# A transformer block on one Trainium2 core: the opening put in order by hand, the end by halves

## The chip, the core and the metric

The kernel runs on one core of a Trainium2 chip. The core has a matrix engine (TensorE, PE in the profile; its weight loads are listed as PEld), a vector engine (VectorE, DVE), a scalar engine (ScalarE, ACT), a general engine (GpSimd, POOL) and a queue for transfers (SyncE, SP). Each engine executes its own instructions strictly in the order in which the program issues them, and semaphores join them. Data stands in SBUF, matrix products arrive in PSUM, and transfers run on 16 DMA engines; SP issues nearly all of them here, and ACT can issue them too. An engine that issues a transfer waits first for the semaphores that the transfer needs, and what is queued behind it waits as well.

The metric is the device time of one execution in microseconds (us). An execution of the kernel before takes 1185.17 us, the median of three runs.

## The reference

The block normalises x (2048 tokens of 576 numbers, no learned scale), and adds to x two branches that both read the normalised x: attention over eight keys at distances 0, 2, ... 14 in 32 heads of 18, and a feed-forward layer of 4608 with a ReLU.

```python
def reference(A_x, A_wqkv, A_wo, B_x, B_w1, B_w2):
    def _A_ref(x, wqkv, wo):
        ...
        qkv = (lambda x, *d: x.transpose(*d))((x @ wqkv).reshape(B, S, 3, H, Dh), 2, 0, 3, 1, 4)
        ...
        attn = _softmax(logits, axis=-1)
        o = jnp.einsum("bhsw,bhswd->bhsd", attn, vg)
        return (lambda x, *d: x.transpose(*d))(o, 0, 2, 1, 3).reshape(B, S, D) @ wo

    def _B_ref(x, w1, w2):
        h = jnp.einsum("bsd,df->bsf", x, w1)
        zero = jnp.zeros_like(h)
        h = jnp.maximum(h, zero)
        return jnp.einsum("bsf,fd->bsd", h, w2)

    x = A_x
    xn = _layernorm(x, axis=-1)
    return x + _A_ref(xn, A_wqkv, A_wo) + _B_ref(xn, B_w1, B_w2)
```

All inputs are float32.

## The kernel before

**Precision.** Products run in fp32r. So each operand is split into a high half, a copy of type fp32r made by ACT, and a low half, the difference of the number and its high half, made by DVE. A product is three products: high by high, low by high, high by low. The 576 rows of the contraction are four blocks of 128 and a rest of 64; the rest's high and low halves share one block of 128 rows. `TERMS` (L294) lists the 14 products of one output tile as pairs of an x block and a weight block: four high by high, four x-low by weight-high, one for the rest, then five with the weight's low half.

**Tiling.** The tokens come in two phases (even and odd ones). A phase has 1024 tokens: eight token tiles of 128, or four blocks `tb` of 256. The feed-forward layer has 36 blocks of 128 hidden units, three to a chunk, 12 chunks. A slot is one hidden block on one token block; `slots` (L464) runs over phases, chunks, token blocks and the three blocks of a chunk. So slots 0 to 2 are token block 0 (token tiles 0 and 1), slots 3 to 5 block 1 (tiles 2 and 3), 6 to 8 block 2, 9 to 11 block 3.

**A slot's work.** `h_mm(n)` (L467) makes the 14 first products into the PSUM tile `ph`, 256 columns each; ACT takes their ReLU as the high half `hhi` and DVE the low half `hlo`. `o_mm(n)` (L482) makes 12 second products of 288 columns into two PSUM tiles `po`, one for each token tile; after the third slot of a chunk DVE adds the sums to x's tile (L500), and after the last chunk `done` sends the tile out on SP's queue (L461). `ps_o` has two buffers, `ps_h` two, `ps_m` two.

**A token tile's way.** `load_x` brings it in; `stats` (L239) takes mean and variance on DVE, and the negative mean and the root on POOL (L249, L250); `norm` (L254) normalises, on DVE in one instruction or on ACT in two (L258, L259), and ACT copies the last 64 columns once more beside themselves (L263); `make_xt` (L285) transposes it by five products (L275, L276) and splits the transposed tile into its high half (ACT, L278, L280) and low half (DVE, L279, L281). A block's first products need both of its tiles transposed and split.

**Weights.** W1, W2, wqkv and wo come through four staging tiles `st` of 640 columns. `stage_more` loads up to three ahead on SP's queue; `run_splits(n)` splits what is due by step n with `two` (L143): the high half on ACT, the low half on DVE. The due steps of the first chunk are `HEADW` (L32); those of the first wqkv tiles begin at step 2. A W1 tile is loaded by three transfers: 256 KB and twice the 32 KB of the rest's 64 rows.

**The order.** The program is written in the order of its issue: at step n it runs due splits, `h_mm(n + 2)`, the work that `at` has put there, `o_mm(n)`, the work that `late` has put there, and attention's DVE work as far as two counters of modelled time for PE and DVE allow. The opening (L555 to L577) loads x and the first weights, prepares token tiles 0 to 2, and puts tiles 3 to 7 into steps -2 to 5 by the table `HEAD` (L34). The attention's first products (qkv) begin at step 7. 24 transposes of a constant tile (L105) run on PE while the first data is on its way.

Of the kernel before, what the change touches and what calls it, by code (L numbers as in the profile page):

```python
# [17 lines left out]
P = 128  # L18
# [13 lines left out]
HEADW = (-5, -2, -1, 0, 0, 1)  # L32

HEAD = (  # L34
    (-2, 0, 'stats', 3),
    (-2, 1, 'xt', 2, True),
    (-1, 0, 'stats', 4),
    (-1, 1, 'norm', 3, True),
    (0, 0, 'xt', 3, False),
    (0, 0, 'norm', 4, True),  # L40
    (0, 0, 'stats', 6),
    (0, 1, 'stats', 5),
    (1, 1, 'norm', 5, False),
    (1, 1, 'xt', 4, False),
    (2, 1, 'xt', 5, False),
    (2, 1, 'norm', 6, True),
    (2, 1, 'stats', 7),
    (4, 0, 'norm', 7, True),
    (4, 1, 'xt', 6, False),
    (5, 1, 'xt', 7, False),  # L50
# [6 lines left out]
def tile_body(ctx: ExitStack, tc: tile.TileContext, x, wqkv, wo, w1, w2, out):  # L57
# [77 lines left out]
    def run_splits(n):  # L135
        while staged and staged[0][0] <= n:
            _, split, st = staged.popleft()
            split(st)
            stage_more()

    held = None

    def two(hi, lo, src, n):  # L143
        def rest():
            nc.vector.tensor_tensor(lo, src, f32(hi), op=ALU.subtract)  # L145
            dve(n)

        nc.scalar.activation(hi, src, AF.Copy)  # L148
        if held is None:
            rest()  # L150
        else:
            held.append(rest)
# [3 lines left out]
    def w1_task(step, key, f):  # L156
        def load(st):
            c = slice(f * P, (f + 1) * P)
            nc.sync.dma_start(
                st[:, 0:512].rearrange("p (k c) -> p k c", k=KT),  # L160
                w1[0 : KT * P, c].rearrange("(k p) c -> p k c", p=P),
            )
            nc.sync.dma_start(st[0:DR, 512:640], w1[KT * P : D, c])
            nc.sync.dma_start(st[DR:P, 512:640], w1[KT * P : D, c])

        def split(st):
            w = w1p.tile([P, 2, 5 * P], F32R, name="w1t")
            two(w[:, 0, :], w[:, 1, :], st[:, :], 640)
            W1[key] = w

        split_task(step, load, split)

    def w2_task(step, key, f):
        def load(st):
            nc.sync.dma_start(st[:, 0:D], w2[f * P : (f + 1) * P, :])
# [78 lines left out]
    def norm(ph, i, act=False):  # L254
        nm, r = MR.pop((ph, i))
        xn = tmp.tile([P, 640], F32, name="xn", bufs=3)
        if act:
            nc.scalar.activation(xn[:, 0:D], X[ph, i], AF.Identity, bias=nm)  # L258
            nc.scalar.activation(xn[:, 0:D], xn[:, 0:D], AF.Copy, scale=r)  # L259
        else:  # L260
            nc.vector.tensor_scalar(xn[:, 0:D], X[ph, i], nm, r, op0=ALU.add, op1=ALU.mult)
# [4 lines left out]
    def transpose_split(src, last, hi, mix, lo, free=False):  # L266

        if free:
            pa, pb = (ps_o.tile([P, 2, 512], F32, name="po")[:, 0, :] for _ in range(2))
            pa, pb = pa.rearrange("p (k c) -> p k c", k=KT), pb[:, 0:P]  # L270
        else:
            pa = ps_m.tile([P, KT, P], F32, name="pm")
            pb = ps_m.tile([P, P], F32, name="pm")
        for k in range(KT):
            nc.tensor.transpose(pa[:, k, :], src[:, k * P : (k + 1) * P], ident)  # L275
        nc.tensor.transpose(pb, last, ident)  # L276
        t["pe"] += 5 * 0.06
        nc.scalar.activation(hi, pa, AF.Copy)  # L278
        nc.vector.tensor_tensor(lo, pa, f32(hi), op=ALU.subtract)  # L279
        nc.scalar.activation(mix, pb, AF.Copy)  # L280
        nc.vector.tensor_tensor(mix[DR:P], pb[DR:P], f32(mix[DR:P]), op=ALU.subtract)  # L281
        dve(512)
        dve(128)

    def make_xt(ph, i, free=False):  # L285
# [5 lines left out]
        transpose_split(xn[:, 0:512], xn[:, 512:640], d[:, 0:4, :], d[:, 4, :], d[:, 5:9, :], free)  # L291
# [175 lines left out]
    def h_mm(n):  # L467
        ph, c, tb, f = slots[n]
        w, xt = W1[ph, c, f], XT[ph, tb]
        pt = ps_h.tile([P, TBN], F32, name="ph")  # L470
        for j, (a, b) in enumerate(TERMS):
            wb = w[:, b // 5, (b % 5) * P : (b % 5 + 1) * P]
            mm(pt, wb, xt[:, a, :], j == 0, j == len(TERMS) - 1, TBN)
# [7 lines left out]

    def o_mm(n):  # L482
        ph, c, tb, f = slots[n]
        hi, lo = H.pop(n)
        w = W2[ph, c, f]
        for k in range(2):
# [3 lines left out]
            for j, (l, b) in enumerate(((hi, 0), (hi, 1), (lo, 0))):  # L490
                for h in range(2):
                    mm(
                        PO[k][:, h, 0:D2], l[:, cs], w[:, b, h * D2 : (h + 1) * D2],
                        f == 0 and j == 0, f == C - 1 and j == 2, D2,
                    )
        if f == C - 1:
# [57 lines left out]

    load_x(0, 0, 2)  # L555
    load_x(0, 1)
    for i in range(1, AHEAD + 1):
        stage_more(i)
        load_x(0, 1 + i)
    for i in range(AHEAD + 2, NI):  # L560
        load_x(0, i)
    stats(0, 0)
    stats(0, 1)
    held = []
    run_splits(-5)
    norm(0, 0)
    norm(0, 1)
    stats(0, 2)
    make_xt(0, 0)
    make_xt(0, 1, True)  # L570
    for f in held:
        f()
    held = None
    run_splits(-LAG)
    norm(0, 2, True)
# [3 lines left out]
    for n in range(-LAG, len(slots)):  # L579
# [38 lines left out]
```

## Time and profile before

| | us |
|---|---|
| median of three runs | 1185.17 (1184.52 to 1185.62) |
| the profiled execution, its own time | 1184.46 |
| its span, first to last instruction | 1182.7 |
| PE busy in the span | 1174.6 |
| DVE busy | 822.3 |
| ACT busy | 306.9 |
| POOL busy | 40.1 |
| first product of h_mm(0) | 9.11 |
| first product of h_mm(6) | 31.54 |
| last product's end | 1178.72 |
| last add's end | 1179.51 |
| last output's issue and landing | 1179.54, 1181.65 |

Times are from the start of the span. The execution's own time is 1.8 us longer than the span, for what lies around it. A row of the timeline gives start, duration, engine, line, operation, and out<-in with partitions and elements. A row of the groups gives the count after x, then the busy time in us, the mean of one in ns, and the idle time before them with what ended it. The chain of waits is followed back from the last instruction: at each step to what released it.

### The profile page before, as it was taken

The numbers are of one execution on the slowest core, as the hardware profiler recorded it, in microseconds if no ns is written. First come the engines' busy times: TensorE is split into PE (matmuls) and PEld (weight loads), VectorE is DVE, ScalarE is ACT, GpSimd is POOL, SyncE is SP. The second block draws the span as 40 slices with busy tenths as digits, with TensorE's granted clock in tenths as the row PEclk, the third lists the DMA queues.
The fourth block names the chain that finished last, engine by engine and source line by source line (L and its number), as shares of the span: only waits on it lengthen the run. The fifth ranks groups of instructions, "written<-read, shape, count | busy, mean of one in ns | idle before, by whom it ended". The sixth has DMA issues, their size and how long they took to land.

```text
span 1182.7 us, 21731 instructions
## 1 busy us (share of the span) xinstructions
PE 1174.6 (99%) x8936; PEld 1164.9 (98%) x8936; DVE 822.3 (70%) x1301; ACT 306.9 (26%) x758; POOL 40.1 (3%) x63
## 2 busy tenths in 40 slices
PE   8999999999999999999999999999999999999998
PEld 8999999999999999999999999999999999999998
DVE  7516885888687668877673288758777884787852
ACT  5422222131222211322233123121322222222210
POOL 2000000010000000000020000000100000000000
PEclk9999999999999999999999999999999999999999
DMA  5312121130312211356342122121302213114541
GB/s 174 85 32 79 39 84 47 47 108 1 99 45 58 65 55 44 104 112 148 105 131 74 47 55 80 32 77 27 98 21 80 70 43 89 47 30 110 115 100 60
DMA packets 137364, 86.16 MB, mean 73 GB/s; under 512 B 48832, under 2 KB 120768, under 8 KB 137264
## 3 DMA queue, kind: packets, MB, share of 16 engines
q1 hardware_dynamic: 134736, 76.58, 24.0%
q10 hardware_dynamic: 2528, 8.20, 2.4%
q8 instruction: 70, 1.15, 0.4%
q14 instruction: 30, 0.25, 0.1%
HBM read 66.58 MB, written 9.96 MB: 65 GB/s over the span
## 4 chain that ended last, share of the span: by engine, by line
PE 95%; DVE 2%; DMA 2%; ACT 0%; SPq 0%; issue 0%; POOL 0%; DVEq 0%; ACTq 0%
PE ph L114 37%; PE po L114 37%; PE pm L114 20%; DMA st<-in_w 1%; DMA xn<-turned 1%; PE pm L275 0%; DVE pr L382 0%; DMA turned<-tr 0%; DVE x L500 0%; DMA x<-in_x 0%; DVE pr L345 0%; SPq L424 0%; DVE w1t L145 0%; DVE w2t L145 0%; DVE bst L245 0%
## 5 line engine op out<-in xcount | busy, mean ns | idle before, releaser
L114 PE MATMUL ph<-xT,w1t 128*128 128x256 f32 x4032 | 513.0, 278 | 1.3 <-ACT xT L278 0.6
L114 PEld LDWEIGHTS ph<-xT,w1t 128*128 128x128 f32 x4032 | 491.9, 188 | 2.1 <-ACT xT L278 0.8
L114 PE MATMUL po<-w2t,hhi 128*128 128x288 f32 x2304 | 400.7, 296 | 0.6 <-DVE w2t L145 0.3
L114 PEld LDWEIGHTS po<-w2t,hhi 128*128 128x128 f32 x2304 | 336.9, 188 | 2.4 <-issue 0.5
L476 ACT ACTIVATE hhi<-ph 128x256 fp32r<-128x256 f32 x288 | 110.1, 382 | 553.5 <-PE ph L114 538.2
L114 PE MATMUL po<-w2t,hlo 128*128 128x288 f32 x1152 | 244.7, 293 | 0.0
L477 DVE SCALAR_TENSOR_TENSOR hlo<-ph,hhi 128x256 fp32r<-128x256 f32 x288 | 121.5, 422 | 161.0 <-ACT hhi L476 160.1
L500 DVE TENSOR_TENSOR x<-po,x 128x576 f32<-128x576 f32 x192 | 143.4, 756 | 69.9 <-PE po L114 67.0
L114 PE MATMUL pm<-wq,xT 128*128 128x432 f32 x896 | 185.5, 358 | 0.0
L114 PEld LDWEIGHTS po<-w2t,hlo 128*128 128x128 f32 x1152 | 183.6, 188 | 0.0
L114 PEld LDWEIGHTS pm<-wq,xT 128*128 128x128 f32 x896 | 163.8, 188 | 5.6
L145 DVE TENSOR_TENSOR w2t<-st,w2t 128x576 fp32r<-128x576 f32 x72 | 54.3, 755 | 45.6 <-ACT w2t L148 45.4
L345 DVE TENSOR_TENSOR pr<-qo,k 128x1152 f32<-128x1152 f32 x64 | 85.8, 1349 | 0.0
L348 DVE TENSOR_REDUCE lg<-pr 128x64 f32<-128x1152 f32 x64 | 84.9, 1343 | 0.0
L375 DVE TENSOR_TENSOR pr<-lg,v 128x1152 f32<-128x1152 f32 x64 | 84.7, 1350 | 0.2
L382 DVE TENSOR_TENSOR pr<-pr 128x288 f32<-128x288 f32 (+1 forms) x128 | 70.6, 601 | 0.1
L145 DVE TENSOR_TENSOR w1t<-st,w1t 128x640 fp32r<-128x640 f32 x72 | 59.0, 820 | 13.8 <-ACT w1t L148 13.7
L148 ACT ACTIVATE w2t<-st 128x576 fp32r<-128x576 f32 x72 | 49.1, 683 | 57.2 <-PE po L114 42.4
L314 ACT ACTIVATE k<-pm 128x144 f32<-128x144 f32 x64 | 18.6, 291 | 143.9 <-PE pm L114 143.9
L148 ACT ACTIVATE w1t<-st 128x640 fp32r<-128x640 f32 x72 | 53.0, 736 | 11.4 <-DMA st<-in_w 11.4
L351 POOL TENSOR_SCALAR_AFFINE_SELECT lg<-lg 1x512 f32<-1x512 f32 x8 | 9.4, 1171 | 844.1 <-DVE lg L348 844.1
L114 PE MATMUL pm<-wq,oT 128*128 128x288 f32 x224 | 35.2, 296 | 0.3 <-ACT oT L438 0.3
(61 smaller groups left out, 444.7 us busy)
## 6 DMA issues: line engine op xcount, KB each, us to landing
st<-in_w SPq DMA_DIRECT2D x72, 288.0 KB, 3.0
st<-in_w SPq DMA_DIRECT2D x72, 256.0 KB, 3.0
st<-in_wqkv SPq DMA_DIRECT2D x32, 216.0 KB, 3.0
turned<-tr SPq DMA_DIRECT2D x64, 80.0 KB, 2.3
xn<-turned SPq DMA_DIRECT2D x16, 320.0 KB, 3.2
st<-in_w SPq DMA_DIRECT2D x144, 32.0 KB, 2.7
out<-x SPq DMA_DIRECT2D x16, 288.0 KB, 2.1
x<-in_x SPq DMA_DIRECT2D x15, 288.0 KB, 3.6
```

The source lines that it names most:

```text
L114: nc.tensor.matmul(o, l, r, start=start, stop=stop)
L145: nc.vector.tensor_tensor(lo, src, f32(hi), op=ALU.subtract)
L148: nc.scalar.activation(hi, src, AF.Copy)
L314: nc.scalar.activation(k[:, W - 1 + i, :], pq[:, 1, :], AF.Copy)
L345: nc.vector.tensor_tensor(pr[i], q, window(k, i), op=ALU.mult)
L348: nc.vector.tensor_reduce(lg[:, i], pr.pop(i).rearrange(heads, d=Dh), axis=AX.X, op=ALU.add)
L351: nc.gpsimd.affine_select(out=z, in_=z, pattern=[[1, NI], [1, W], [0, HG]], compare_op=ALU.is_ge, fill=-1e9 / scale, base=1 - W, channel_m ...
L375: nc.vector.tensor_tensor(pr[i].rearrange(heads, d=Dh), e, window(v, i).rearrange(heads, d=Dh), op=ALU.mult)
L382: nc.vector.tensor_tensor(o, z[:, 0:n], z[:, n : 2 * n], op=ALU.add)
L476: nc.scalar.activation(hi, pt, AF.Relu)
L477: nc.vector.scalar_tensor_tensor(lo, pt, 0.0, f32(hi), op0=ALU.max, op1=ALU.subtract)
L500: nc.vector.tensor_tensor(acc, PO[k][:, :, 0:D2], acc, op=ALU.add)
```

## The change

**The opening is written out by hand**, up to `o_mm(3)` and the transposes of token tile 5; the loop begins at step `FIRST` = 4, and `HEAD` keeps tiles 6 and 7, one step later than before for their transposes.

- The first products of slots 0 and 1 take turns by kind of term (`h_terms`): high by high of slot 0, x-low of slot 0, high by high and x-low of slot 1, then the remaining six of slot 0 and of slot 1. Slot 2's products follow, into a tile of the pool of `po`.
- The second W1 tile is loaded by ACT's queue, behind a small ACT instruction that reads the first half of x's tile 0.
- Token tile 0 is normalised on ACT, tile 1 on DVE; tiles 2 and 3 on DVE by another instruction (`beside`: the root as a second tensor operand).
- The second products of slots 0, 1 and 2 stand ahead of slot 3's first products: `o_mm(0)`, `o_mm(1)`, the transposes of tile 3, `o_mm(2)`, `h_mm(3)`, the transposes of tile 4.
- The low halves of the first two W1 tiles, of the last two W2 tiles of chunk 0 and of two wqkv tiles are made by POOL (`by_pool`) and no longer by DVE.
- The copies of the last 64 columns (L263) go; the transposed rest has 64 rows, and its low half is written from them to the other 64 rows.

**The end.** In the last slot the second products of a token tile are ordered by column half, and each half is added and sent out by itself, the first halves on SP's queue, the second on ACT's.

```diff
-HEADW = (-5, -2, -1, 0, 0, 1)
+HEADW = (-9, -8, -7, -6, -5, -4)
+FIRST = 4
...
+    (4, 0, 'stats', 6),
+    (4, 1, 'norm', 6, True),
+    (4, 1, 'stats', 7),
+    (5, 0, 'norm', 7, True),
+    (5, 1, 'xt', 6, False),
+    (6, 1, 'xt', 7, False),
...
     def two(hi, lo, src, n):
...
+        nc.scalar.activation(hi, src, AF.Copy)
+        if step_now in by_pool:
+            nc.gpsimd.tensor_tensor(lo, src, f32(hi), op=ALU.subtract)
+        else:
             nc.vector.tensor_tensor(lo, src, f32(hi), op=ALU.subtract)
             dve(n)
...
+        elif beside:
+            nc.vector.scalar_tensor_tensor(xn, X[ph, i], nm, r.to_broadcast([P, D]), op0=ALU.add, op1=ALU.mult)
+            dve(600)
...
-        nc.scalar.activation(xn[:, D:640], xn[:, KT * P : D], AF.Copy)
...
+        if end:
+            for k in range(2):
                 for h in range(2):
...
+                    z = X[ph, 2 * tb + k][:, h * D2 : (h + 1) * D2]
+                    nc.vector.tensor_tensor(z, PO[k][:, h, 0:D2], z, op=ALU.add)
+                    (nc.scalar if h else nc.sync).dma_start(o_v[ph, 2 * tb + k][:, h * D2 : (h + 1) * D2], z)
...
+    by_pool.update((-9, -8, -5, -4, 2, 3))
+    both, x_low, w_low, last = TERMS[0:4], TERMS[4:8], TERMS[9:13], [TERMS[8], TERMS[13]]
     load_x(0, 0, 2)
     load_x(0, 1)
...
+    stage_more(1)
+    nc.scalar.activation(spare, X[0, 0][:, 0:1], AF.Copy)
+    queue = nc.scalar
+    stage_more(2)
+    queue = nc.sync
+    load_x(0, 2)
+    stage_more(4)
+    for i in (3, 4, 5):
         load_x(0, i)
     stats(0, 0)
+    norm(0, 0, True)
     stats(0, 1)
+    norm(0, 1)
+    x0 = make_xt(0, 0, parts=True)
+    x0[0]()
+    run_splits(-9)
+    x1 = make_xt(0, 1, True, parts=True)
+    x1[0]()
+    x0[1]()
+    x1[1]()
+    h_terms(0, both)
+    run_splits(-8)
+    load_x(0, 6)
+    load_x(0, 7)
+    stats(0, 2)
+    for z in x0[2:], x1[2:]:
+        for f in z:
+            f()
+    h_terms(0, x_low)
+    h_terms(1, both)
+    h_terms(1, x_low)
+    h_terms(0, w_low + last)
+    h_terms(1, w_low + last)
+    run_splits(-7)
+    norm(0, 2, beside=True)
+    h_out(0)
+    h_terms(2, TERMS, True)
+    h_out(1)
+    run_splits(-6)
+    make_xt(0, 2)
+    h_out(2)
+    stats(0, 3)
+    o_mm(0)
+    run_splits(-5)
+    norm(0, 3, beside=True)
+    o_mm(1)
+    run_splits(-4)
+    make_xt(0, 3)
+    stats(0, 4)
+    norm(0, 4, True)
+    o_mm(2)
+    run_splits(2)
+    h_mm(3)
+    stats(0, 5)
+    make_xt(0, 4)
+    norm(0, 5, True)
+    h_mm(4)
+    run_splits(3)
+    h_mm(5)
+    o_mm(3)
+    make_xt(0, 5)
...
-    for n in range(-LAG, len(slots)):
+    for n in range(FIRST, len(slots)):
```

`h_out(n)` is the second part of `h_mm`: the ReLU on ACT and the low half on DVE. `x0` and `x1` are the four steps of a token tile after its transposes: high half, low half, and the same of the rest. `AHEAD`, the staging tiles and the pools are as before.

More of the change, by code (lines that the diff above doesn't have):

```diff
@@ L271, in transpose_split @@
         else:
             pa = ps_m.tile([P, KT, P], F32, name="pm")
-            pb = ps_m.tile([P, P], F32, name="pm")
+            pb = ps_m.tile([P, P], F32, name="pm")[0:DR]
         for k in range(KT):
             nc.tensor.transpose(pa[:, k, :], src[:, k * P : (k + 1) * P], ident)
-        nc.tensor.transpose(pb, last, ident)
+        nc.tensor.transpose(pb, src[:, KT * P : D], ident)
         t["pe"] += 5 * 0.06
-        nc.scalar.activation(hi, pa, AF.Copy)
-        nc.vector.tensor_tensor(lo, pa, f32(hi), op=ALU.subtract)
@@ L280, in transpose_split, with high, low, last_high @@
[L280 to L285, printed above, removed]
+        def high():
+            nc.scalar.activation(hi, pa, AF.Copy)
+        def low():
+            nc.vector.tensor_tensor(lo, pa, f32(hi), op=ALU.subtract)
+            dve(512)
+        def last_high():
+            nc.scalar.activation(mix[0:DR], pb, AF.Copy)
+        def last_low():
+            nc.vector.tensor_tensor(mix[DR:P], pb, f32(mix[0:DR]), op=ALU.subtract)
+            dve(128)
@@ L286, in make_xt @@
+        steps = high, low, last_high, last_low
+        if not parts:
+            for f in steps:
+                f()
+        return steps
+    def make_xt(ph, i, free=False, parts=False):
         tb, h = divmod(i, 2)
```

106 lines of the change are left out of this document (44 added, 62 removed).

## The prediction

> Short names: T(i) is the five transposes of token tile i, h(n) the 14 first products of slot n (wide, `ph`), o(n) its 12 second products (`po`); "the mark" is the first product of h(6). Durations are rows of the profiled execution, in us; sums by me say so.
>
> **What bounds it now.** First the chain that ended last by share, then the same chain in order of time, to see where TensorE stops waiting.
>
> ```profile
> PE 95%; DVE 2%; DMA 2%; ACT 0%; SPq 0%; issue 0%; POOL 0%; DVEq 0%; ACTq 0%
> ```
>
> ```profile
> 19.42 1.59 PE po L114 x10
> 21.01 1.61 PE ph L114 x14
> ```
>
> From 19.42 on the chain is TensorE alone until the last add, so the time is TensorE's fixed work plus what it loses in the first 20 us and after its last product. An o costs 1.59, an h 1.61, a T 0.55 (0.44 + 0.11 in that chain). Then windows of 3.41 us, for the clock (columns: busy time and instructions of PE, weight loads, DVE, ACT, POOL; granted clock; DMA).
>
> ```profile
> 7.24:10.66 3.42, 2.10 (x14) 1.42 (x13) 3.26 (x9) 3.28 (x10) 0.75 (x2) 1.00 0.96 257
> 10.66:14.07 3.41, 3.41 (x16) 3.19 (x16) 2.17 (x5) 1.50 (x4) 0.00 (x0) 0.50 0.95 314
> 14.07:17.48 3.41, 3.27 (x28) 3.08 (x27) 3.25 (x9) 2.85 (x6) 0.75 (x2) 1.00 0.64 250
> 17.48:20.90 3.42, 3.06 (x21) 2.39 (x20) 3.22 (x8) 3.30 (x9) 1.35 (x2) 1.00 0.28 74
> ```
>
> A window in which PE was 61% busy is followed by one at half clock (a 256-wide product then takes 0.213 instead of 0.114, start to start); 89% busy is followed by full clock. Last, the timeline and the groups, for the steps between transposes and products, and for POOL.
>
> ```profile
> 7.67 0.58 ACT L278 ACTIVATE xT<-pm 128x512 fp32r<-128x512 f32 x1
> ...
> 8.63 0.68 DVE L279 TENSOR_TENSOR xT<-pm,xT 128x512 fp32r<-128x512 f32 x1
> ...
> 17.23 0.81 DVE L245 BATCH_NORM_STATS2 bst<-x 128x6 f32<-128x288 f32 x2
> ...
> 22.73 0.57 POOL L250 TENSOR_TENSOR rstd<-mv,mhalf 128x1 f32<-128x1 f32 x1
> ...
> 31.54 1.66 PE L114 MATMUL ph<-xT,w1t 128*128 128x256 f32 x13
> ```
>
> ```profile
> L351 POOL TENSOR_SCALAR_AFFINE_SELECT lg<-lg 1x512 f32<-1x512 f32 x8 | 9.4, 1171 | 844.1 <-DVE lg L348 844.1
> L307 POOL MEMSET v<- 1x1008 f32 x8 | 7.5, 931 | 0.0
> ```
>
> 31.54 is the mark; T(0) to T(5), h(0) to h(5), o(0) to o(3) lie before it, and in the changed program the same work does. So the change is worth its shift of the mark, plus new waits behind the mark, plus the end.
>
> **To the end of T(2).** ACT now issues the second W1 tile: it waits for x's first half (landed 2.94), issues two, and its third issue has to wait for a semaphore of the first W1 tile's 256 KB (landed 5.52). No ACT issue lies in this stretch; SP's took 0.43 to 0.59, ACT's halo issues (L320) 0.56 to 1.36: I take 0.6, so ACT is free at 6.15 (up to 6.9). The normalisation of tile 0, on ACT now, takes 0.78 + 0.10 + 0.78 (L258, L259): 7.85, against 6.42 on DVE before. T(0) and T(1) start there. ACT then does tile 0's high half (0.59 from 8.65), W1's (0.74), tile 1's (0.59), with starts overlapped by 0.08 as in the timeline: first product at 10.45, 1.3 later than before (9.11). Taking the kinds of terms in turn then does its work: 42 products and a wait of 0.2 for tile 1's low half. PE is about 40% busy in 7.24 to 10.66, so by the row above the next window is at half clock: 16 products to 14.07, 26 more at 0.114 to 17.0, T(2) to 17.5. The low halves of W1 that POOL makes come in time even at 1.5 each (from 9.9: 11.4 and 12.9). What is left to the mark is 3 T, 3 h, 4 o = 1.65 + 4.83 + 6.36 = 12.84. Without any further wait the mark lies at 30.34: a gain of 1.20.
>
> **Wait A, second products.** POOL's queue is in order, and the low half of the second W2 tile stands in it behind the mean and root of tile 3, because `stats(0, 3)` is written ahead of `run_splits(-5)`. Those wait for DVE, whose queue holds tile 2's low halves and h(2)'s low half first. From the end of T(2): tile 2's high half on ACT 0.64 with its handoff, low 0.74, last rows 0.33, hlo(2) 0.45, statistics 0.82 + 0.21 + 0.15 and gaps 1.31, root on POOL 0.66, the W2 split 1.37: 5.50. PE has o(0) and two products of o(1) to do, 1.59 + 0.26; inside, the second half of o(0) also waits for hlo(2), which frees its PSUM tile. PE loses 3.65. The POOL split of 128x576 is in no row: between 0.53 (by the memset, 0.92 ns an element) and 1.9 (the affine select's 2.29 ns an element, 1.32, plus the 0.57 that a one-column tensor_tensor takes). I take 1.32, since the affine select reads and writes too.
>
> **Wait B, T(4).** Tile 4's statistics stand on DVE behind tile 3's low halves, so from the end of T(3): 0.64 + 0.74 + 0.33 + 1.31 + 0.66, then 1.69 on ACT and 0.05: 5.42 until T(4), covered by o(2) and h(3), 3.20. PE loses 2.22. Before, `stats` of 4 was done at 18.5.
>
> **Waits C and D.** T(5) stands directly ahead of h(6), and T(7) ahead of h(9); before, h(5) and o(3), or h(8) and o(6), lay between. In the first products of before the step from the last transpose to the first product was 0.74 (8.37 to 9.11); the next four products wait some 0.17 more for the low half: 0.92 each.
>
> **Clock.** A leaves PE some 40% busy in 20.9 to 24.3, so the window after it runs at half clock: T(3) takes 1.07 instead of 0.55, on the path: 0.55 (0 if the clock stays; 1.6 if the window before is slow too and o(1) with it). The Trainium skill (TensorE: Matmul & The Clock Gate, What's actually happening) has the gate close after an idle window; by that the term is 0 and the sum 1191.1, but the 61% row speaks against it, so the row is used.
>
> **Hidden.** The 16 copies of 64 columns that go (L263, 0.26 each), wq's two splits on POOL and wider normalisations on DVE lie beside PE; DVE has room (9.1 of 10.6 busy to the mark). If that cover were gone the last would cost 0.2 each. On SP the loads of x(6), x(7) and of the third W2 tile now stand behind the second W2 load, which waits for a staging tile that POOL's first split frees (11.4); with the 2.5 to 5.9 from issue to landing seen up to 30 us they are there by 18 to 19, and used after 22.
>
> **The end.** All adds of a token tile wait for its last product, so halves can't start sooner: four adds of 128x288 at 0.45 (L453) against two of 0.76 end 0.33 later. The last output lands 2.1 after its issue (both of the last two did); a half may take less (x: 2.2 against 3.0). Between -0.5 and +0.35; I take +0.2.
>
> **Sum.** -1.20 + 3.65 + 2.22 + 0.92 + 0.92 + 0.55 + 0.2 = +7.26 on 1184.46, this execution's own time (span 1182.7): 1191.7. The three runs lie at 1184.5 to 1185.6, median 1185.17.
>
> **Rivals.**
> - *Port.* Once the root of tile 3 is there, POOL's W2 split and DVE's new normalisation, which reads x and r from SBUF, start together. If one must wait for the other, POOL loses up to 0.76 (the 128x576 row of L145), on A: 1192.5. For: the starts coincide. Against: no row of before overlaps such a pair. The Trainium skill (SBUF — State Buffer, Who interferes with whom) has it as a rule: an instruction of DVE with two SBUF inputs and one of GpSimd that reads SBUF exclude each other for their whole length. No run here shows it yet.
> - *Loads.* Two queues share the engines, the first W1 tile lands up to 0.8 later (one 256 KB load's landing after another's), ACT is held and everything shifts: 1192.5. For: DMA 0.96 busy in 7.24 to 10.66.
> - *Full clock.* No half-clock window at all: 1.6 less before T(2) and 0.55 less after: 1189.5. Against: before had one.
> - *A covered.* If POOL's piece is ready in time, PE has no idle window, and B, C and D stay: 3.06, 1187.5.
> - *Not slower.* PE never waits after T(2) for the chain ACT, DVE, POOL: it decides if that chain takes 1.85 or less to the W2 split and 3.2 or less to T(4), where I have 5.5 and 5.4. Then A, B and the clock term go: +0.84, 1185.3; with C and D hidden too, 1183.5. Handoffs of 0.04 speak for speed, the in-order queues against.
> - That the turns of terms don't happen is ruled out by the order of instructions on PE: four, four, four, four, six, six.
>
> **Chances.** Forecast 0.48, port 0.15, loads 0.12, full clock 0.10, A covered 0.05, not slower 0.10. 0.2% is 2.4 us, about what a measurement here tells from no change: slower has the first four and half of "A covered", whose time lies on the bound, 0.88; same the other half and 0.06 of the last, 0.08; faster its other 0.04. The forecast's own bounds (POOL -0.8/+0.6, ACT's issue, clock -0.55/+1.1, port, end) give 1189.5 to 1195; down to 1187.5 it takes in the full clock and part of "A covered".
>
> **What would show it.** First product near 10.4; PE idle about 1 us inside o(0) until hlo(2), then until POOL's W2 subtraction, in all 3.6; T(4) waiting for ACT's xn; waits of 0.7 before h(6) and h(9); the mark at 37 to 38.5; PE dense after h(9). I am wrong if POOL's W2 split ends before 20, or the mark lies before 34.

## The result, and the profile after

The changed kernel takes 1192.68 us, the median of five runs (1191.79 to 1194.94), beside 1185.47 (1184.52 to 1185.62) of the kernel before in the same comparison: 1.0069 times as long by the comparison's estimate, interval 1.0057 to 1.0082 (the quotient of the two medians is 1.0061). The profiled execution is the one of 1192.68; its span is 1190.9.

First the shares of the chain that ended last, from the page, and the longest piece of that chain:

```profile
PE 80%; issue 10%; DVE 4%; DMA 4%; ACT 1%; SPq 0%; POOL 0%; POOLq 0%; DVEq 0%; ACTq 0%
```

```profile
952.27 104.92 issue
```

TensorE had 95% of it before, but the fall to 80% is not lost time. Nearly all of the "issue" share is this one piece, in which the chain follows POOL's queue while POOL is idle, and TensorE is busy for all of its 104.92 us; the profile of the repeat (e1) has 95% again. What TensorE waits for is read from the timeline. Next that of the changed kernel, for the places where TensorE waits in the opening (start, duration, engine, line, operation, out<-in, count, and in brackets the idle time before and what ended it). In its numbering L269 is the transposes, L105 all products, L493 `hlo`, L253 the normalisation with the root as a tensor, L141 a subtraction on POOL, L251 the second half of a normalisation on ACT.

```profile
10.62 3.73 PE L105 MATMUL ph<-xT,w1t 128*128 128x256 f32 x28 [1.14 <-ACT xT L274]
...
16.25 1.07 PE L105 MATMUL po<-w2t,hhi 128*128 128x288 f32 x4
18.56 0.80 PE L105 MATMUL po<-w2t,hhi 128*128 128x288 f32 x4 [0.98 <-DVE hlo L493]
19.75 0.58 POOL L242 TENSOR_TENSOR rstd<-mv,mhalf 128x1 f32<-128x1 f32 x1
20.29 3.30 POOL L141 TENSOR_TENSOR w2t<-st,w2t 128x576 fp32r<-128x576 f32 x2
20.36 1.94 DVE L253 SCALAR_TENSOR_TENSOR xn<-x,nm,rstd 128x576 f32<-128x576 f32 x1 [0.70 <-POOL rstd L242]
21.75 0.53 PE L105 MATMUL po<-w2t,hhi 128*128 128x288 f32 x2 [1.86 <-POOL w2t L141]
...
29.02 0.66 PE L269 MATMUL pm<-ident,xn 128*128 128x128 f32 x4 [0.37 <-ACT xn L251]
35.77 2.15 PE L105 MATMUL ph<-xT,w1t 128*128 128x256 f32 x14 [0.58 <-ACT xT L274]
47.63 2.18 PE L105 MATMUL ph<-xT,w1t 128*128 128x256 f32 x14 [0.58 <-ACT xT L274]
```

The waits stand in the order that was forecast: T(0) and the first product; inside o(0) for slot 2's low half; for POOL's W2 split; T(4); h(6); h(9). The prediction's "mark", the first product of h(6), lies at 35.77, 4.23 later than before. The DVE row of 1.94 is new: the same instruction on tile 2 took 0.82.

The clock, in windows (time, then busy time and instructions of PE, weight loads, DVE, ACT, POOL; granted clock, DMA share, GB/s):

```profile
6.20:9.61 3.41, 1.65 (x13) 1.14 (x11) 0.93 (x4) 2.30 (x4) 0.76 (x2) 1.00 0.93 277
9.61:13.03 3.42, 2.41 (x18) 2.22 (x19) 2.87 (x9) 2.62 (x6) 2.87 (x2) 1.00 0.90 284
...
19.85:23.26 3.41, 1.55 (x12) 1.52 (x12) 1.94 (x1) 0.00 (x0) 3.41 (x3) 1.00 0.08 10
23.26:26.68 3.42, 3.42 (x17) 3.38 (x16) 1.80 (x4) 0.76 (x2) 0.33 (x1) 0.50 0.43 122
```

There is no half-clock window at the start this time, and one right behind the wait for POOL.

Last, a place that nothing in the prediction names. Two views: a piece of the chain of waits (start, duration, what), and the timeline around it; L167 is the load of a W2 tile, L139 its high half, L143 its low half, L531 the addition to x that frees a `po` tile.

```profile
839.56 5.62 DMA st<-in_w
```

```profile
845.27 0.69 ACT L139 ACTIVATE w2t<-st 128x576 fp32r<-128x576 f32 x1 [1.67 <-DMA st<-in_w]
845.98 0.76 DVE L143 TENSOR_TENSOR w2t<-st,w2t 128x576 fp32r<-128x576 f32 x1 [1.74 <-ACT w2t L139]
846.99 1.41 DVE L531 TENSOR_TENSOR x<-po,x 128x576 f32<-128x576 f32 x2
847.89 0.78 PE L105 MATMUL po<-w2t,hhi 128*128 128x288 f32 x4 [1.11 <-DVE x L531]
```

A W2 tile lands 5.62 after its issue. ACT and DVE wait for it; behind its low half stands the addition that frees the tile which the next second products need, and TensorE waits 1.11. Two more such waits lie at 263.36 (0.32) and 1084.66 (0.85). In the kernel before the two others are absent, and the first is 0.14 long: the same load and the products behind it, in the chain of before, are

```profile
833.40 4.64 DMA st<-in_w
840.75 1.80 PE po L114 x12
```

So the chain of before already ran through this load. The prediction's sentence that from 19.42 on the chain is TensorE alone holds for the two ends of it alone: in between the chain leaves TensorE near 501, 574, 820 and 1085. The 2% of DMA in the line that it shows first, some 20 us, could not all lie in the opening.

So the sum of this execution is: slot 40's ReLU, long after the opening, is 5.82 later than before; the last product's end is 8.15 later; what lies behind it is 0.07 longer (4.02 against 3.95 to the span's end). 5.82 + 2.33 + 0.07 = 8.22, the difference of the two profiled times (1192.68 and 1184.46).

### The profile page after: what moved, and what is told of

Same layout as the page of the kernel before. It is cut to its first block, busy times and chain, and to the rows that moved or that the text cites. A ratio compares the mean times of both kernels' runs of the same rounds, so it can differ in the third digit from the quotient of the medians.

```text
span 1190.9 us, 21729 instructions
## 1 busy us (share of the span) xinstructions
PE 1175.4 (99%) x8936; PEld 1164.8 (98%) x8936; DVE 819.1 (69%) x1297; ACT 304.4 (26%) x743; POOL 47.4 (4%) x69
## 4 chain that ended last, share of the span: by engine, by line
PE 80%; issue 10%; DVE 4%; DMA 4%; ACT 1%; SPq 0%; POOL 0%; POOLq 0%; DVEq 0%; ACTq 0%
PE po L105 31%; PE ph L105 31%; PE pm L105 18%; DMA st<-in_w 2%; PE pm L269 1%; DVE x L531 1%; DMA xn<-turned 1%; DMA st<-in_wo 0%; DVE pr L353 0%; DVE pr L390 0%; DVE w1t L143 0%; DMA turned<-tr 0%; DVE hlo L493 0%; DVE w2t L143 0%; DVE lg L356 0%
## 5 line engine op out<-in xcount | busy, mean ns | idle before, releaser
L105 PE MATMUL ph<-xT,w1t 128*128 128x256 f32 x4018 | 510.1, 278 | 2.3 <-ACT xT L274 2.3
L105 PEld LDWEIGHTS ph<-xT,w1t 128*128 128x128 f32 x4018 | 489.3, 188 | 3.7 <-ACT xT L274 3.1
L105 PE MATMUL po<-w2t,hhi 128*128 128x288 f32 x2304 | 402.3, 296 | 5.1 <-DVE x L531 2.3
L105 PEld LDWEIGHTS po<-w2t,hhi 128*128 128x128 f32 x2304 | 338.0, 189 | 7.4 <-ACT hhi L492 2.3
L105 PE MATMUL po<-w2t,hlo 128*128 128x288 f32 x1152 | 245.4, 294 | 0.0
L493 DVE SCALAR_TENSOR_TENSOR hlo<-ph,hhi 128x256 fp32r<-128x256 f32 x287 | 120.6, 421 | 164.3 <-ACT hhi L492 163.6
L531 DVE TENSOR_TENSOR x<-po,x 128x576 f32<-128x576 f32 x190 | 142.2, 756 | 66.9 <-PE po L105 64.0
L105 PE MATMUL pm<-wq,xT 128*128 128x432 f32 x896 | 185.5, 358 | 0.0
L105 PEld LDWEIGHTS po<-w2t,hlo 128*128 128x128 f32 x1152 | 184.2, 188 | 0.0
L105 PEld LDWEIGHTS pm<-wq,xT 128*128 128x128 f32 x896 | 163.8, 188 | 5.6
L143 DVE TENSOR_TENSOR w2t<-st,w2t 128x576 fp32r<-128x576 f32 x70 | 52.7, 753 | 45.5 <-ACT w2t L139 45.4
L143 DVE TENSOR_TENSOR w1t<-st,w1t 128x640 fp32r<-128x640 f32 x70 | 57.3, 819 | 13.1 <-ACT w1t L139 12.9
L139 ACT ACTIVATE w2t<-st 128x576 fp32r<-128x576 f32 x72 | 49.3, 684 | 61.6 <-PE po L105 44.4
L139 ACT ACTIVATE w1t<-st 128x640 fp32r<-128x640 f32 x72 | 52.9, 735 | 7.2 <-DMA st<-in_w 7.1
L105 PE MATMUL pm<-wq,oT 128*128 128x288 f32 x224 | 35.3, 297 | 0.3
```

Of the source, the lines that this page charges most:

```text
L105: nc.tensor.matmul(o, l, r, start=start, stop=stop)
L493: nc.vector.scalar_tensor_tensor(lo, pt, 0.0, f32(hi), op0=ALU.max, op1=ALU.subtract)
L531: nc.vector.tensor_tensor(acc, PO[k][:, :, 0:D2], acc, op=ALU.add)
```

## The experiments

"Shift" below is how much later than in the profile of before slot 40's ReLU starts: what the opening costs in that one execution, without anything that comes later. Half-clock windows are those before 40 us. "Later waits" sums PE's idle pieces over 0.15 after 60 us; 0.42 of it, at the change of phase, is in every kernel.

| kernel | shift | half clock from | later waits | median (range), us | ratio to before |
|---|---|---|---|---|---|
| before | 0 | 10.66 | 0.68 | 1185.47, 1184.43, 1184.94, 1184.12 | 1 |
| changed | 5.82 | 23.26 | 2.70 | 1192.68 (1191.79 to 1194.94) | 1.0069 (1.0057 to 1.0082) |
| e1_repeat | 7.98 | 7.71, 11.12, 24.78 | 1.07 | 1193.48 (1189.92 to 1195.29) | 1.0071 (1.0049 to 1.0094) |
| e2_cover | 4.16 | 22.60 | 1.32 | 1189.97 (1189.11 to 1192.89) | 1.0051 (1.0035 to 1.0067) |
| e3_split_first | 4.63 | none | 0.57 | 1190.61 (1189.16 to 1192.14) | 1.0052 (1.0037 to 1.0067) |
| e6_sp_queue | 5.43 | 20.73 | 1.30 | 1190.51 (1189.94 to 1192.43) | 1.0054 (1.0039 to 1.0069) |
| e5_w2_on_dve | 4.15 | none | 2.17 | 1189.46 (1188.36 to 1190.66) | 1.0044 (1.0031 to 1.0058) |
| e8_norm3_plain | 7.21 | 10.34, 23.99 | 2.12 | 1193.69 (1193.13 to 1194.24) | 1.0074 (1.0056 to 1.0093) |
| e7_covers_joined | 1.77 | none | 1.09 | 1187.79 (1186.94 to 1188.72) | 1.0024 (1.0015 to 1.0033) |
| e4_end_only | 0.46 | 11.18 | 0.77 | 1184.75 (1183.70 to 1186.59) | 0.9999 (0.9990 to 1.0008) |
| e9_old_second_order | -0.82 | none | 2.55 | 1184.05 (1182.52 to 1185.60) | 0.9993 (0.9984 to 1.0001) |
| e11_changed_five | 5.82 | 22.21 | 1.58 | 1190.93 (1190.76 to 1193.16) | 1.0062 (1.0050 to 1.0075) |
| e12_before_five | -0.68 | none | 0.42 | 1183.70 (1183.45 to 1185.02) | 0.9997 (0.9988 to 1.0006) |
| e10_five_staging | -0.88 | none | 0.42 | 1182.81 (1182.42 to 1183.44) | 0.9990 (0.9981 to 0.9999) |

The four medians of before belong to the comparisons of the changed kernel, of e1, e2, e3 and e6, of e4, e7, e8 and e9, and of e5, e10, e11 and e12, in this order. The ratios are the comparisons' own estimates and can differ a little from the quotient of two medians.

### e1: the changed kernel once more

No edit.

> The changed kernel once more, for a second profile and for the waits behind the opening: in its first profile TensorE waits 0.32, 1.11 and 0.85 us at 263, 848 and 1085 us for the adds of L531 on DVE, which stand behind a split of W2 whose data landed late; the kernel before has none. Theory: transfers land up to 1 us earlier or later from execution to execution, and after the shift some slack is used up, so these waits will be there in another number or at other places: 0 to 4 of them, and a time of 1191 to 1195. Rival: they belong to the changed program, and come back at the same three places with the same sizes.

The waits of the opening came back at the same places (1.28 for `hlo`, 1.85 for POOL, 0.68 for T(4), twice 0.58). The clock did not; the windows of this execution:

```profile
4.30:7.71 3.41, 1.31 (x12) 1.06 (x10) 1.82 (x6) 1.13 (x2) 1.51 (x4) 1.00 0.90 270
7.71:11.12 3.41, 2.40 (x10) 1.91 (x10) 0.69 (x1) 2.15 (x5) 0.48 (x1) 0.50 0.89 254
11.12:14.54 3.42, 3.27 (x15) 3.28 (x16) 3.09 (x8) 1.75 (x5) 3.42 (x4) 0.50 0.85 276
```

Two half-clock windows at the start, none in the first profile: the opening is 2.16 longer. Of the three later waits only the one near 848 came back, with 0.65. One execution's total is not the kernel's; its waits are.

### e2: T(5) and T(7) a second product earlier (waits C and D)

```diff
-    (4, 0, 'stats', 6),
-    (4, 1, 'norm', 6, True),
-    (4, 1, 'stats', 7),
-    (5, 0, 'norm', 7, True),
-    (5, 1, 'xt', 6, False),
-    (6, 1, 'xt', 7, False),
+    (4, 0, 'norm', 7, True),
+    (4, 1, 'xt', 6, False),
+    (5, 1, 'xt', 7, False),
...
+    stats(0, 6)
     h_mm(5)
+    make_xt(0, 5)
+    norm(0, 6, True)
+    stats(0, 7)
     o_mm(3)
-    make_xt(0, 5)
```

> Changed kernel, but with the transposes of tile 5 ahead of o(3), those of tiles 6 and 7 one step earlier, and the statistics and normalisations of tiles 6 and 7 moved ahead to fit. Theory (waits C and D, transposes directly ahead of the products that need them): the two waits of 0.58 for ACT's high half before h(6) and h(9), and the 0.5 more inside these products, go, 2.2 us in all; about half comes back, since tile 5's normalisation is then waited for (0.5) and its low half too (0.6): 1.1 us under the changed kernel, 1191.5. Rival: the waits are only moved, as DVE and ACT have as much to do: no change, 1192.7.

Both waits of 0.58 are gone. The 14 products of h(9) take 1.78 instead of 2.18, as those of h(6) did before; those of h(6) still take 2.04 (2.15 in the changed kernel), and T(5) now waits 0.19. The shift falls by 1.66, with the half-clock window of wait A still there: C and D cost this together. That is more than the 1.1 that was expected, of which the wait for T(5) was to take 0.5 and the low half 0.6.

### e3: the second W2 tile's splits ahead of tile 3's statistics

```diff
+    run_splits(-5)
     stats(0, 3)
     o_mm(0)
-    run_splits(-5)
     norm(0, 3, beside=True)
```

> Changed kernel, but with the split of the second W2 tile ahead of tile 3's statistics in the program, so that POOL makes its low half before tile 3's mean and root. Theory (wait A is POOL's order): POOL's split begins at about 18.0, when ACT's high half is there, and ends at 19.5 instead of 21.7; the 1.86 us wait for POOL inside o(1) goes, the 0.98 before o(0)'s second half stays. T(4)'s wait for its normalisation grows from 0.4 to some 1.6 as it loses cover, and the window at half clock may go (up to 1.5 more): 0.6 to 2.7 us under the changed kernel, 1190.7 most likely. Rival: o(1) waits for something else as well (the tile's landing, ACT's high half), then the wait stays and the time is 1192.7.

From the timeline of e3, the first rows of transposes behind o(0):

```profile
18.54 0.80 PE L105 MATMUL po<-w2t,hhi 128*128 128x288 f32 x4 [0.97 <-DVE hlo L493]
22.45 0.63 PE L269 MATMUL pm<-ident,xn 128*128 128x128 f32 x4 [1.25 <-DVE xn L253]
27.96 0.66 PE L269 MATMUL pm<-ident,xn 128*128 128x128 f32 x4 [1.58 <-ACT xn L251]
```

The wait of 1.86 for POOL is gone, and so is the half-clock window. In its place T(3) waits 1.25 for tile 3's normalisation and T(4) 1.58 instead of 0.37: 2.83 where 2.23 were. Yet the shift is 1.19 smaller: the window of 3.41 us at half clock, 1.71 us of lost work, had cost more than the difference of 0.60. With that window gone, T(4)'s wait is seen at its size, and the small 0.37 is explained: slow products had covered it.

### e5: the low halves of W2 on DVE

```diff
-    by_pool.update((-9, -8, -5, -4, 2, 3))
+    by_pool.update((-9, -8, 2, 3))
```

> The changed kernel with the low halves of the second and third W2 tile made by DVE instead of POOL. Theory (POOL's part of A is the queue: its split stands behind tile 3's root and takes 1.42): DVE makes the split right behind tile 3's statistics, near 19.7 to 20.5, a wait of about 0.6 takes the place of 1.86, and the normalisation of tile 3 takes 0.82 again; 1.3 less than the changed kernel (range 0.5 to 2.0), that is 1191 to 1192.5. Rival (the chain over POOL is not what holds T(3) and T(4)): a new wait for T(3) or T(4) as large as the gain, time unchanged within 0.5.

```profile
19.68 0.77 DVE L143 TENSOR_TENSOR w2t<-st,w2t 128x576 fp32r<-128x576 f32 x1
19.83 1.05 POOL L242 TENSOR_TENSOR rstd<-mv,mhalf 128x1 f32<-128x1 f32 x1
20.50 0.53 PE L105 MATMUL po<-w2t,hhi 128*128 128x288 f32 x2 [0.53 <-DVE w2t L143]
20.91 0.82 DVE L253 SCALAR_TENSOR_TENSOR xn<-x,nm,rstd 128x576 f32<-128x576 f32 x1 [0.47 <-POOL rstd L242]
...
27.41 0.66 PE L269 MATMUL pm<-ident,xn 128*128 128x128 f32 x4 [1.58 <-ACT xn L251]
```

0.53 takes the place of 1.86, as expected, T(3) does not wait, no half-clock window follows, and T(4) waits its 1.58. Shift -1.67. The 1189.46 lies below the 1191 to 1192.5 that was expected, but the kernel before was faster too in this comparison: against its own kernel before, median by median, the changed kernel loses 7.21, e3 6.18 and e5 5.34, so that e5 wins 1.87, inside the expected 0.5 to 2.0. The intervals of e5 and of the changed kernel hardly touch (1.0058 and 1.0057), those of e3 and the changed kernel overlap.

### e6: the second W1 load on SP's queue

```diff
-    queue = nc.scalar
     stage_more(2)
-    queue = nc.sync
```

> Changed kernel, but with the second W1 tile loaded on SP's queue as before. Theory: ACT no longer waits at its third issue for the first W1 tile (until 5.93), starts tile 0's normalisation when x's statistics are there (about 5.0 instead of 6.47), and the first product moves from 10.62 to about 9.7; the whole opening shifts by 0.7 to 1.0 us: 1191.8. Rival: the first W1 tiles then land late enough to hold the products, or the later waits take it back: 1192.7.

The first product comes at 9.26 instead of 10.62, since ACT no longer stands behind its third issue. The lead lasts through wait A (the product behind POOL starts at 20.40, not 21.75). But the shift is only 0.39 smaller, where 0.7 to 1.0 was expected. In this execution the half-clock window, from 20.73, lies on o(1) and T(3), so T(3) starts only 0.46 earlier, and T(4), whose chain begins behind it, waits 1.35 where it waited 0.37. Without such a window, in e7, the lead stays: T(3) and T(4) start 1.33 earlier there than in e3.

### e7: e2, e3 and e6 together

> The changed kernel with three edits together: the transposes of tiles 5 and 7 a second product earlier (C, D), the splits of the second W2 tile ahead of tile 3's statistics (POOL's part of A), the second W1 load on SP's queue. Theory (the excess is the named waits of the opening, which hand over to each other): C and D give about 2.2, the SP queue 1.4, and of POOL's 1.86 only the part that the next waits for T(3) and T(4) don't take, some 0.5 to 1.5; the mark comes 4 to 5 earlier than in the changed kernel, near 32 to 33; time 1187 to 1189. Rival (the single gains measured add, -3.5, -2.9 and -3.0 against the repeat): 1184 or below. Rival (opening is not the cause, the later waits are): no better than the best of the three alone, 1190.

```profile
21.12 0.63 PE L266 MATMUL pm<-ident,xn 128*128 128x128 f32 x4 [1.27 <-DVE xn L250]
26.63 0.66 PE L266 MATMUL pm<-ident,xn 128*128 128x128 f32 x4 [1.58 <-ACT xn L248]
```

1187.79 is inside 1187 to 1189. The rival's 1184 did not come; it had summed the three gains against the repeat, which lost 9.05 against its own kernel before, where the first comparison has 7.21. By the shifts the three edits win 1.66, 1.19 and 0.39 alone, 3.24 in all, and 4.05 together: alone, e3 and e6 each give about 1 us back to a longer wait for T(4) (1.58 and 1.35 for 0.37), and together they give it back once. So the waits do hand over to each other. What is left is o(0)'s wait for `hlo` (1.01), T(3)'s (1.27) and T(4)'s (1.58). h(6)'s first product is at 32.97.

### e8: tile 3 normalised by the form with one tensor input

```diff
-    norm(0, 3, beside=True)
+    norm(0, 3)
```

> The changed kernel with tile 3 normalised by the tensor_scalar form (one tensor input) instead of the form with the root as a second tensor input. Theory (DVE's two-input instruction and POOL's W2 subtraction exclude each other, the 1.94 of that instruction being 0.8 of work and 1.1 of waiting for POOL): the normalisation takes 0.6 to 0.9 beside the same POOL subtraction of about 1.4, which is not longer; time as the changed kernel's to 0.5, since DVE's wait was hidden. Rival (POOL slows any DVE instruction that reads SBUF): again 1.5 or more. Rival (DVE's wait was on the path): 0.7 or more faster, with T(3) or T(4) that much earlier.

```profile
7.05 0.58 DVE L256 TENSOR_SCALAR xn<-x,nm,rstd 128x576 f32<-128x576 f32 x1 [0.70 <-POOL rstd L242]
21.46 3.00 POOL L141 TENSOR_TENSOR w2t<-st,w2t 128x576 fp32r<-128x576 f32 x2
21.54 1.65 DVE L256 TENSOR_SCALAR xn<-x,nm,rstd 128x576 f32<-128x576 f32 x1 [0.70 <-POOL rstd L242]
```

The first rival's number came: the form with one tensor input takes 1.65 beside POOL's subtraction and 0.58 alone (tile 1), 1.07 more; the form with two took 1.94 against 0.82, 1.12 more. The theory that only two inputs bring the exclusion falls. The rival's wording, any DVE instruction that reads SBUF, is too wide all the same: in the changed kernel's profile the statistics of tile 2 take their usual 0.81 in the middle of two POOL subtractions.

```profile
10.16 3.09 POOL L141 TENSOR_TENSOR w1t<-st,w1t 128x640 fp32r<-128x640 f32 x2 [3.03 <-DMA st<-in_w]
11.21 0.81 DVE L237 BATCH_NORM_STATS2 bst<-x 128x6 f32<-128x288 f32 x2
```

No time was won in e8, so DVE's wait was hidden, as expected of it.

### e4: the kernel before with the end by halves alone

```diff
+            if end:
+                terms.sort(key=lambda z: z[3])
...
+        if end:
+            for k in range(2):
+                for h in range(2):
...
+                    nc.vector.tensor_tensor(z, PO[k][:, h, 0:D2], z, op=ALU.add)
+                    (nc.scalar if h else nc.sync).dma_start(o_v[ph, 2 * tb + k][:, h * D2 : (h + 1) * D2], z)
```

> The kernel before with the end by halves alone. Theory (the term of +0.2): all four half adds still follow the last product; four of 0.45 against two of 0.76 end about 0.3 later, a half output lands a little sooner; from the last product's end to the last add's end about 0.85 instead of 0.79; time within -0.5 to +0.35 of the kernel before, that is 1184.0 to 1184.8 beside 1184.4. Rival (the halves bring an overlap): faster by 0.6 or more. Second rival (an output issue on ACT's queue is slower): slower by 0.6 or more.

The row of the adds: `x4` stands for four in a row, the first of which starts 0.76 before the last product's end, at 1179.49.

```profile
1178.73 1.62 DVE L503 TENSOR_TENSOR x<-po,x 128x288 f32<-128x288 f32 x4 [3.15 <-PE po L114]
```

The last add ends at 1180.35, 0.86 after the last product (0.79 before), and the last output lands 1.86 after its issue (2.11 before). The ratio's interval is 0.1% to both sides of 1: what the end by halves is worth can't be told from nothing.

### e9: the changed first products, the old order behind them

The turns of terms, POOL's W1 low halves, the missing copies and the end stay; the second W1 load is on SP; from slot 2 on the order of the kernel before, with its table `HEAD` from step 0 on.

```diff
-HEADW = (-9, -8, -7, -6, -5, -4)
-FIRST = 4
+HEADW = (-9, -8, -7, 0, 0, 1)
+FIRST = 0
...
-    by_pool.update((-9, -8, -5, -4, 2, 3))
+    by_pool.update((-9, -8))
...
-    run_splits(-7)
-    norm(0, 2, beside=True)
+    norm(0, 2, True)
+    stats(0, 3)
     h_out(0)
-    h_terms(2, TERMS, True)
+    run_splits(-7)
     h_out(1)
-    run_splits(-6)
     make_xt(0, 2)
-    h_out(2)
-    stats(0, 3)
-    o_mm(0)
...
     stats(0, 4)
-    norm(0, 4, True)
-    o_mm(2)
...
+    norm(0, 3, True)
```

> The changed kernel's first products (turns by kind of term for slots 0 and 1, W1's low halves by POOL, no copies of 64 columns, the end by halves, second W1 load on SP) with the order of the kernel before from slot 2 on: h_mm(2), T(3), o_mm(0) and so on, W2's low halves on DVE, the loop from step 0. Theory (the loss is A to D, all in the order of the second products and transposes 2 to 7, and the turns themselves cost nothing): no wait over 0.7 between 12 and 55 us, the mark at 31.5 to 33, time 1184 to 1186, within 1.5 of the kernel before. Rival (the turns by term or the loads lose by themselves): 1188 or more. Rival (the turns gain as much as they were counted for, 1.2): 1183.2. On the later waits near 848 and 1085: if they come with the late opening, they are absent here; if with the changed kernel's loop as such, they are here too.

```profile
14.71 1.89 PE L111 MATMUL ph<-xT,w1t 128*128 128x256 f32 x14 [0.63 <-DVE hlo L499]
18.57 0.54 PE L111 MATMUL po<-w2t,hhi 128*128 128x288 f32 x2 [0.81 <-DVE w2t L149]
```

1184.05: all of the change's loss is gone with its order from slot 2 on, which is the main point of the case. (The low halves of W2 and wqkv went back to DVE with it, and the second W1 load left ACT's queue, which alone was worth 0.39 in e6's shift.) One of the waits, 0.81, is above the 0.7 that was allowed, and the mark at 30.73 is ahead of the 31.5 to 33 expected. The turns themselves lose nothing that can be measured. That they gain is not shown: the shift of -0.82 is that of an execution without a half-clock window, and e12, with the old first products and no such window either, has -0.68. Near 842 this profile has the largest of all later waits, 1.65, so these do not come with a late opening.

### e11, e12, e10: a fifth staging tile

One edit to the changed kernel (e11), the kernel before (e12) and e9 (e10); the opening's order stays.

```diff
-    stp = pool("stp", 4)
+    stp = pool("stp", 5)
...
-    def stage_more(ahead=AHEAD):
-        while tasks and len(staged) < ahead:
+    def stage_more(ahead=None):
+        while tasks and len(staged) < (ahead or AHEAD):
...
+    AHEAD = 4
     for n in range(FIRST, len(slots)):
```

The reason lies in the profiles taken so far. The wait near 845 and the time from issue to landing of the W2 tile in front of it, for eleven of them:

| kernel | e4 | before | e3 | e7 | e6 | e2 | e5 | e1 | e8 | changed | e9 |
|---|---|---|---|---|---|---|---|---|---|---|---|
| issue to landing, us | 4.53 | 4.64 | 4.66 | 4.71 | 4.84 | 5.01 | 5.11 | 5.15 | 5.58 | 5.62 | 6.15 |
| PE's wait, us | under 0.15 | under 0.15 | 0.15 | 0.21 | 0.33 | 0.51 | 0.61 | 0.65 | 1.08 | 1.11 | 1.65 |

The wait is the landing time less 4.50, to 0.01, in all nine that have one: this tile has no slack, whichever way the opening is written. (The three were planned from the profiles of before to e9; e5 ran with them.)

> The changed kernel with a fifth staging tile, and one load more ahead from the loop's start on; the opening's order is as it was. Theory (the waits after 60 us are the landing of one load that has no slack, its time from issue to landing less 4.5): no wait over 0.25 for a W2 split near 263, 848 and 1085; opening waits unchanged; 0.6 to 2.3 less than the changed kernel's 1192.7 to 1193.5, that is 1190.5 to 1192.3. Rival (the waits come from contention among the transfers, which an earlier load only moves): waits of the same size elsewhere after 60 us, time unchanged within 0.5.

> The kernel before with the same fifth staging tile. Theory (the load without slack is there too, with 4.6 from issue to landing in the two profiles of this opening, a wait of 0.14 or less): 0 to 0.5 less, 1184.4 to 1185. Rival (the late landings are as frequent here as in the changed kernel, and the profiles seen were lucky ones): 0.6 to 1.5 less, about 1183.5 to 1184.3; then the later waits are no part of what the change costs. Second rival: the earlier loads collide with the attention's transfers, 0.5 or more slower.

> The changed first products with the old order of the second products, the end by halves, and the fifth staging tile. Theory: the wait of 1.65 near 842 in its profile goes and so does 0.48 near 257; 0.5 to 1.7 less than 1184.05, that is 1182.4 to 1183.5, which is faster than the kernel before by 0.1 to 0.2%. Rival (contention): 1184.05 to 0.4.

In all three profiles no wait for a W2 split over 0.15 is left after 60 us. The load itself also lands sooner, after 2.97 to 3.15 instead of 4.53 to 6.15: in the eleven it is the third of three loads issued within 1.4 us, with the fifth tile no longer. So slack and a lighter queue of transfers came together, and what each is worth was not separated. e11's opening waits are the old ones but for T(4)'s (0.86 for 0.37), its shift is 5.82 as in the changed kernel's profile, and its last product's end 5.88 later than before instead of 8.15. Its 1190.93 is 1.75 and 2.55 below the two medians of the changed kernel, inside the expectation, though the intervals overlap; one later wait is larger than before (1.16 at 1101.89, for attention's last tile; 0.26 in the kernel before). e12 gives 0.4, inside the theory's 0 to 0.5 and no difference that is measured. e10 gives 1182.81, inside its 1182.4 to 1183.5, ratio 0.9990 with an interval that ends at 0.9999: if it is faster than the kernel before, then by 0.1%. With thirteen kernels compared, one interval that ends so close to 1 is weak evidence, and 0.1% is under the 0.2% that the prediction took as the bound. Against e12 (1183.70) the intervals overlap, so how much of it is the turns stays open.

## Why the prediction was right, point by point

It forecast 1191.7, and 1192.68 came, for the reason it gave: an order that puts second products and transposes directly behind the chain that feeds them. e9 shows this whole, e2, e3 and e5 in parts. That the total came so near is in part luck: the start won 1.25 more than forecast, and 2.33 of later waits had not been forecast at all. The terms one by one:

- **Start, -1.20.** Right in sign, too small in this profile. ACT was free at 6.47, not 6.15, since the first W1 tile landed at 5.93 instead of 5.52 under two loading queues (the "loads" rival, half its size); first product 10.62 instead of 10.45. But the half-clock window that the sum had from 10.66 did not come (the first half of the "full clock" rival), and o(0) started at 16.25 instead of 17.5. With the 12.84 that is left to the mark the start was worth -2.45. In the repeat, with two such windows, o(0) started at 18.13, which makes -0.57.
- **Wait A, 3.65.** Right in place, length and releaser. From T(2)'s end to the product that waited for POOL: 16.25 to 21.75, the 5.50 of the sum. POOL's subtraction is 1.42 in e7, where it stands alone (1.32 was taken between 0.53 and 1.9). PE was idle 0.98 + 1.86 = 2.84 in it; the rest of the 3.65, 0.81, lies in products that took longer than 1.85 in all, those of the first half of o(0) above all.
- **Wait B, 2.22, and the clock, 0.55.** Together near right, in the parts wrong. The window behind A did run at half clock, in all six profiles that keep A whole, and in none of the five in which POOL's split comes earlier or DVE makes it (e3, e5, e7, e9, e10). The rule of the Trainium skill that was weighed here (TensorE: Matmul & The Clock Gate, What's actually happening), by which the term was 0, asks for an idle window; a window 45% busy was enough. But it held T(3) and o(2), 17 products, not T(3) alone: 3.41 us at half clock are 1.71 us of lost work, where the sum had 0.55. o(2) is part of the cover of T(4)'s chain, so T(4) waited only 0.37: 2.08 in all against 2.77. Where the window falls differs, and T(4)'s wait with it: 0.37 to 1.35 in the six. Without the window the wait is 1.58 (e3, e5, e7).
- **Waits C and D, 0.92 each.** Right: e2 wins 1.66 with both. 0.58 ahead of the product and some 0.4 inside.
- **The end, +0.2.** Inside its bounds and not to be told from zero (e4).
- **Port, a rival at 0.15.** The exclusion exists, and its price falls on the other engine: POOL started at 20.29, DVE at 20.36, and DVE waited, with nothing behind it that was late (then POOL's next subtraction took 1.95, for 1.42 in e3). In e5 it is the other way round: DVE's subtraction started at 19.68, and POOL's root, 0.57 to 0.58 otherwise, took 1.05. The Trainium skill (SBUF — State Buffer, Who interferes with whom) has it that whoever issues first holds the shared pair for its whole instruction; both rows agree. "No run here shows it yet" was wrong: in the profile of before POOL's root of one column, 0.57 by itself, takes 1.17 beside DVE's subtraction of a W2 tile.

```profile
18.61 1.43 DVE L145 TENSOR_TENSOR w2t<-st,w2t 128x576 fp32r<-128x576 f32 x2
18.63 1.17 POOL L250 TENSOR_TENSOR rstd<-mv,mhalf 128x1 f32<-128x1 f32 x1
```

- **What was missing.** The three later waits, 2.3 in the profile of the result, have no term in the sum, which expected a dense PE after h(9). In the profile of before the tile that the largest hangs on landed in 4.64, so its wait was 0.14 only; that the tile had no slack stood in the chain of before, in the middle that the prediction took for TensorE alone. So the total came near partly because an opening of 5.82 and 2.33 of later waits make 8.15, where 7.06 and nothing had been forecast. The mark shows it: 37 to 38.5 was expected and 35.77 came.
- **The clock row.** "A window in which PE was 61% busy is followed by one at half clock" was read as a rule from one instance, and is none: the first profile has 48% from 6.20 to 9.61 followed by full clock. Over the fourteen profiles, windows of 46% or less (eight) were always followed by half clock, those of 62% or more in the opening at full clock never, and between 47% and 61% both happened (55% and 61% to half; 47% twice, 48%, 49%, 51%, 54% twice and 61% to full). What decides there is open.

## What to carry to other kernels

An instruction that a matrix product waits for has to be looked up in its engine's queue, not in its own dependences: here a W2 subtraction of 1.4 us cost 1.9 us of TensorE and a clock window because a root for another tile stood ahead of it. Every transpose wants a block of products between itself and the first product that reads it, and every normalisation one between its statistics and its transpose. Waits that follow each other on one chain are not added: with one gone the next grows, so what an edit is worth is seen only with the next ones gone too, and a load whose landing varies by 1.6 us needs that much slack before the absence of its wait from one profile means anything.

## What the runs showed of the hardware that was not expected

- The clock's windows are 3.41 us long and their edges lie elsewhere in each execution: 6.20, 4.30 and 5.14 are edges in three profiles of the same opening (changed, e1, e11). The Trainium skill (TensorE: Matmul & The Clock Gate, What's actually happening) calls the window free-running, which agrees. A stretch with TensorE half idle is then a lottery: no half-clock window at the start in two profiles of that opening, two in the third. The kernel before spread over 3.7 us in 27 runs of one comparison, the changed kernel over 5.4 in four of e1.
- DVE's `TENSOR_SCALAR` with one tensor input, which takes 0.58 for 576 columns, waits for POOL just as the form with two does (e8), while the statistics, which read SBUF too, do not (0.81 beside POOL, 0.82 without). The Trainium skill (SBUF — State Buffer, Who interferes with whom) counts `tensor_scalar` among the operations whose fast modes take the shared pair, which this agrees with; that it is a fast mode is only concluded, from 0.58 against 0.82.
- The same W2 load, at the same place of the program and with the same order of work on DVE around it, took 4.53 to 6.15 from issue to landing. Why it varies was not tried.
